# TensorE sums w_val's low parts, w_out's first piece is loaded and converted later, the last rests get a buffer of their own

## The chip, the cores and the metric

One core of a Trainium2 chip runs the whole program; the other cores are idle. The metric is the device time of one execution in microseconds (us). The kernel before takes 745.67 us in the median of three runs (744.39 to 746.3).

## What is computed

Three layers follow each other for 8 batches of 576 tokens, 512 features (8 heads of 64).

```python
# 1 linear attention with an RMS norm over each head
kv  = einsum('bhsd,bhse->bhde', k, v)
out = einsum('bhsd,bhde->bhse', q, kv)
x   = out / sqrt(mean(out**2, -1) + 1e-6) * g_norm          # heads put side by side
# 2 gate: a causal convolution of 5 taps in time, a product with w_val, w_out
gate = sigmoid(sum_k conv_w[k] * shift(x, k))
y    = (gate * (x @ w_val)) @ w_out
# 3 spatial gating
h    = gelu(y @ w_in); u, v = split(h)
v    = (v - mean(v)) / sqrt(var(v) + 1e-6) * g_ln
out  = y + (u * (w_sg @ v + b_sg)) @ w_out2
```

The weights come as 64-bit floats. TensorE multiplies fp32r operands; to keep precision, every operand is split into a high part (rounded to fp32r) and a low part (the rest), and a product is three matmuls: high by high, low by high, high by low.

## The kernel before

**Layout.** Features lie on the 128 partitions in four pieces (m = 0 to 3), tokens along the free dimension: 512 main tokens of each batch, and the 64 tokens left over ("rests") of four batches together. Layers 1 and 2 run batch by batch and store y to DRAM (y_main, y_rest); layer 3 runs over the batches again.

**Weights of 64 bits.** A piece of w_val or w_out is 128 columns by 512 rows, 512 KB. `split` (line 131) makes its two parts out of the raw words. On ACT, `first` takes the absolute value of the high word (L117) and later a copy rounds the high part into the weight (L162, to WV or WOh). On DVE there are seven steps of 128x512: the sign (L127), a minimum (L128), the high part put together (L120), its exponent (L129), the low word scaled (L124), the high part less its rounded copy (L167), and the sum of the last two, which is the weight's low part (L169, to WV or WOl). `in_turn` (line 657) runs two pieces, step by step in turn. The pieces of w_val and w_out use two scratch buffers (m % 2) in the tile wiv.

**The start of the program**, inside `tc.manual_schedule()`, stands in the order in which it is written: the loads on SP's queue; both pairs of w_val; 40 dummy products (`busy`, L217, tile warm) on TensorE; the k by v products (L252) in two halves; the first piece of w_out; the conv weights (cw); then batch 0's attention. For each of its five token tiles: q by kv (L268, tile o), the square on ACT (L275), its sum over a head (L278) and a scale (L279) on DVE, the power -1/2 on POOL (L280), the scaling on DVE (L283), a transpose on TensorE (L298, tile xT), two copies on ACT (L302, L303), and the low part of x on DVE (L307). After it come the products with w_val (tile val), the convolution (16 steps L332 on DVE, tile G), the gate (L360), the split of the gated value (tile Z: L361, L364), and w_out's second piece.

**Behind it a scheduler** sets the order on every engine, by its own idea of the times. An engine works through its queue in that order. The products with w_out (tile y) need w_out's pieces: y's feature piece m needs the high and low part of piece m. Pieces 2 and 3 of w_out are split in that part, among batch 1's attention and convolution.

**The end.** Layer 3's last step for a batch is `wout2`: 12 matmuls (tile out), DVE adds y to half of it (L586, in the tile Y that y was loaded to), SP stores it (L587). After the last batch the rests of the last four batches follow: y_rest is loaded to Y (L877), of which there is one buffer.

Of the kernel before, what the change touches and what calls it, by code (L numbers as in the profile page):

```python
# [10 lines left out]
F32R = mybir.dt.float32r  # L11
# [8 lines left out]
P = 128  # L20
# [40 lines left out]
def body(ctx, tc, qT, k, v, gcol, w_val, conv_w, w_out, w_in, g_ln, w_sgT, b_sg, w_out2, out, out_r):  # L61
# [8 lines left out]
    def sb(tag, shape, dtype=F32, bufs=1):  # L70
        count[0] += 1
        return pool.tile([P] + shape, dtype, tag=tag, name=f"{tag}_{count[0]}", bufs=bufs)
# [15 lines left out]
    def f32(x):  # L88
        return x.bitcast(F32)
# [4 lines left out]

    ident = sb("ident", [P])
    make_identity(nc, ident)
    mhalf = sb("mhalf", [8])
    nc.gpsimd.memset(mhalf, -0.5)
    kvbd = [sb(f"kvbd{i}", [NK, P]) for i in range(2)]
# [8 lines left out]
    def wide_parts(raw, t):  # L108

        hi, lo = raw[:, :, 1], raw[:, :, 0]
        m, b, s = t[:, 0], t[:, 1].bitcast(I32), t[:, 2].bitcast(I32)

        def first():
            act(m, hi.bitcast(F32), AF.Abs, scale=2.0 ** -112)  # L117

        def high():
            stt(b, m.bitcast(I32), 3, s, op0=ALU.logical_shift_left, op1=ALU.bitwise_or)  # L120
            return f32(b)

        def low():
            stt(m, lo.bitcast(U32), 2.0 ** -52, f32(s), op0=ALU.mult, op1=ALU.mult)  # L124
            return m

        return first, (lambda: ts(s, hi, -0x80000000, None, op0=ALU.bitwise_and),  # L127
                       lambda: ts(m, m, EXP_MAX, None, op0=ALU.min), high,  # L128
                       lambda: ts(s, b, -0x800000, None, op0=ALU.bitwise_and), low)  # L129

    def split(src, h, l, raw=None, tmp=None, k=None, on_pool=True):

        st = {}
        n = src.shape[1] * (k or 1)
        wide = src.dtype != F32

        def flat(x):
            return x.rearrange("p (k n) -> p k n", k=k) if k else x

        def load():  # L140
            r = raw
            if r is None:
                r = sb("raw", [WC * 2], I32 if wide else F32, bufs=2)
            if not wide:
                r = r.bitcast(F32)[:, :n] if raw is not None else r[:, :n]
            st["raw"] = r
            s = src.bitcast(I32) if wide else src
            dma(flat(r), s.rearrange("(k p) n -> p k n", p=P) if k else s)

        def first():  # L150
            if wide:
                st["steps"] = wide_parts(st["raw"].rearrange("p (n t) -> p n t", t=2),
                                         sb("cv", [3, n]) if tmp is None else tmp)
                st["steps"][0]()

        def steps():

            ops = st["steps"][1]
            yield ops[0]()
            yield ops[1]()  # L160
            a = ops[2]()
            act(h, flat(a), AF.Copy)  # L162
            yield
            yield ops[3]()
            c = ops[4]()
            yield
            (nc.gpsimd.tensor_tensor if on_pool else tt)(flat(a), flat(a), f32(h), op=ALU.subtract)  # L167
            yield
            tt(l, flat(a), flat(c), op=ALU.add)  # L169
            yield  # L170

        def rest():
            r = st["raw"]
            if wide:
                for _ in steps():
                    pass
            else:
                act(h, flat(r), AF.Copy)
                tt(l, flat(r), f32(h), op=ALU.subtract)

        def work():
            first()
            rest()

        return load, work, first, steps if wide else lambda: iter([rest()])

    def split_weight(w, src, c0, n):

# [26 lines left out]
    def busy(n):  # L215
        for i in range(n):
            nc.tensor.matmul(warm[:, :P], lhsT=ident, rhs=ident, start=True, stop=True)  # L217
# [411 lines left out]

    spare = sb("Y", [2, 2 * D], I32)  # L630

    def first_weight(w, src, raws):
        return [split(src[:, m * P:(m + 1) * P], w[0][:, :, m * P:(m + 1) * P], w[1][:, :, m * P:(m + 1) * P],
                      raws[m], first[1][:, m % 2], NK, False)
                for m in range(NK)]

    wv_pieces = first_weight((wv[:, 0], wv[:, 1]), w_val, [first[0][:, i] for i in range(4)])
    wo_pieces = first_weight(wo, w_out, [spare[:, 0], spare[:, 1], first[0][:, 0], first[0][:, 1]])
    att = Attention(0)
    atts = [att, Attention(1)]  # L640

# [14 lines left out]

    def in_turn(*pieces):

        for p in pieces:
            p[2]()  # L660
        running = [p[3]() for p in pieces]
        while running:
            running = [r for r in running if next(r, running) is not running]


    with tc.manual_schedule():
        for m in range(NK):
            wv_pieces[m][0]()
        wo_pieces[0][0]()
        att.load_kv()  # L670
        dma(gcol_s, gcol)
        dma(gln_s, g_ln)
        cw_work = taps()
        att.load_q()
        atts[1].load_kv()
        wo_pieces[1][0]()
        atts[1].load_q()
        in_turn(wv_pieces[0], wv_pieces[1])
        in_turn(wv_pieces[2], wv_pieces[3])
        wo_pieces[2][0]()  # L680
        wo_pieces[3][0]()
        busy(40)
        att.kv(0)
        busy(5)
        att.kv(1)
        busy(4)
        in_turn(wo_pieces[0])
        slots.drain()
        cw_work()
        steps = [att.o(t, None) for t in range(5)]  # L690
        lows = []
        for t in range(5):
            steps[t][0](ts)
            if t >= 2:
                steps[t - 2][1]()
                busy(4)
                lows.append(steps[t - 2][2]())
            if t == 4:
                lows[0]()
        for t in (3, 4):  # L700
            steps[t][1]()
            if t == 3:
                busy(4)
                lows.append(steps[t][2]())
            lows[t - 2]()
        lows[3]()
        moe = Moe(att.xh, att.xl, gate, y_main[0])
        steps[4][2]()
        for m in range(NK):
            att.taps(m)  # L710
        z = [moe.val(m, True) for m in (0, 1)]
        atts[1].kv(0)
        atts[1].kv(1)
        slots.drain()
        z += [moe.val(m, True) for m in (2, 3)]
        for a in (0, 2):
            att.conv((a, a + 1))
            att.sigmoid(a)
            att.sigmoid(a + 1)
        for m in range(NK):  # L720
            z[m][0]()
        for m in range(NK):
            z[m][1](False)
        in_turn(wo_pieces[1])
    marks = [latest()]
    atts.append(Attention(2))
    atts[2].load_kv()
# [99 lines left out]
    for b in range(B):  # L827
        more = b + 1 < B
        if b % RG == 0:
            if b:  # L830
                grp = Group(b // RG, Group.load(b // RG))
            ggr = sb("WOh", [2, NK, RW], F32R)
            for m in range(NK):
                grp.hu(m)
                tick()
        gg = sb("Z", [2, NK, MAIN], F32R)
        for m in range(NK):
            u = toks.hu(m)
            tick()
            vs = tmp(S)  # L840
            for c in range(2):
                sg(b, c, m, toks.v, rem[b % 2], vs)
                if c:
                    gated(b, m, vs, u, grp.u, gg, ggr)
                tick()
            if more and m == 2:
                ntoks = Tokens(b + 1)
                ntoks.load(0)
                ntoks.load(1)
        res = sb("Y", [NK, MAIN])  # L850
        for m in range(NK):
            dma(res[:, m], y_main[b][:, m])
        if more:
            nrem = Rests((b + 1) // 2) if b % 2 else None
            for t in range(4):
                ntoks.split(t)
                if t < 2:
                    ntoks.load(t + 2)
                ntoks.hv(t)
                tick()  # L860
                if t:
                    wout2(t - 1, gg, res, out[b])
                    tick()
            if nrem:
                nrem.split()
                rem = nrem.hv()
                tick()
            wout2(3, gg, res, out[b])
            tick()
        else:  # L870
            slots.drain()
            for m in range(NK):
                wout2(m, gg, res, out[b])
                tick()
        if b % RG == RG - 1:
            res = sb("Y", [NK, RW])
            dma(res, y_rest[b // RG])  # L877
            for m in range(NK):
                wout2(m, ggr, res, out_r[b // RG])
                tick()  # L880
        if more:
            toks = ntoks
# [41 lines left out]
```

## Time and profile before

| | |
|---|---|
| median of three runs | 745.67 us |
| the profiled execution | 744.89 us, its span 743.1 us |
| TensorE (PE) busy | 728.1 us, 98% of the span |
| VectorE (DVE) busy | 588.4 us, 79% |
| ScalarE (ACT) busy | 348.5 us, 47% |
| GpSimd (POOL) busy | 151.7 us, 20% |

The 1.8 us between the span and the execution's time lie around the span and are taken as fixed. TensorE is busy nearly all of the span, so time can be won at the two ends, where it waits, and lost wherever it is made to wait in between. DVE is busy almost without a gap from 5 to 82 us.

### The profile page before, as it was taken

The numbers are of one execution on the slowest core, as the hardware profiler recorded it, in microseconds if no ns is written. First come the engines' busy times: TensorE is split into PE (matmuls) and PEld (weight loads), VectorE is DVE, ScalarE is ACT, GpSimd is POOL, SyncE is SP. The second block draws the span as 40 slices with busy tenths as digits, with TensorE's granted clock in tenths as the row PEclk, the third lists the DMA queues.
The fourth block names the chain that finished last, engine by engine and source line by source line (L and its number), as shares of the span: only waits on it lengthen the run. The fifth ranks groups of instructions, "written<-read, shape, count | busy, mean of one in ns | idle before, by whom it ended". The sixth has DMA issues, their size and how long they took to land.

```text
span 743.1 us, 11758 instructions
## 1 busy us (share of the span) xinstructions
PE 728.1 (98%) x4498; PEld 625.8 (84%) x4498; DVE 588.4 (79%) x1137; ACT 348.5 (47%) x662; POOL 151.7 (20%) x163
## 2 busy tenths in 40 slices
PE   8898999999999999999999999999999999999996
PEld 7787788778878787889989889888899888898896
DVE  6899979898879899699985786766866857867662
ACT  3757465565665665465433433324433424334220
POOL 0405537261626281211000010000100000100000
PEclk9999999999999999999999999999999999999999
DMA  9935243623363111443122211221230122111203
GB/s 293 343 131 192 103 146 135 210 82 139 132 224 121 54 71 71 156 150 118 58 70 71 85 66 39 81 86 53 90 128 29 57 86 70 59 58 43 100 1 113
DMA packets 56199, 80.14 MB, mean 108 GB/s; under 512 B 3664, under 2 KB 29264, under 8 KB 55120
## 3 DMA queue, kind: packets, MB, share of 16 engines
q1 hardware_dynamic: 56144, 79.40, 32.0%
q8 instruction: 35, 0.57, 0.3%
q14 instruction: 20, 0.16, 0.1%
HBM read 60.51 MB, written 18.87 MB: 107 GB/s over the span
## 4 chain that ended last, share of the span: by engine, by line
PE 85%; DVE 9%; POOL 2%; DMA 1%; issue 1%; ACT 1%; SPq 0%; DVEq 0%; POOLq 0%
PE sg L560 16%; PE hv L451 13%; PE out L201 12%; PE hu L201 12%; PE val L201 11%; PE y L201 10%; DVE G L332 4%; PE kv L252 3%; PE o L268 3%; PE xT L298 2%; POOL st L280 2%; PE hur L201 2%; DMA wiu<-in_w_val_dram 1%; DVE st L278 1%; DVE wiv L120 1%
## 5 line engine op out<-in xcount | busy, mean ns | idle before, releaser
L332 DVE SCALAR_TENSOR_TENSOR G<-X,cw,G 128x576 f32<-128x576 f32 x128 | 98.8, 819 | 6.5 <-ACT G L326 6.5
L201 PE MATMUL y<-Z,WOh 128*128 128x512 f32 (+1 forms) x320 | 99.7, 383 | 0.0
L463 POOL TENSOR_TENSOR bmv<-bmv,mhalf 128x1 f32<-128x1 f32 x36 | 21.4, 596 | 344.2 <-DVE bmv L462 344.2
L451 PE MATMUL hv<-wiv,X1h 128*128 128x512 f32 x256 | 83.3, 390 | 0.0
L201 PE MATMUL out<-Z,K 128*128 128x512 f32 x256 | 83.1, 389 | 0.0
L201 PE MATMUL hu<-X1h,wiu 128*128 128x512 f32 x256 | 79.4, 391 | 0.0
L280 POOL TENSOR_TENSOR st<-st,mhalf 128x8 f32<-128x8 f32 (+1 forms) x40 | 73.5, 1846 | 26.0 <-DVE st L279 23.5
L201 PEld LDWEIGHTS y<-Z,WOh 128*128 128x128 f32 x320 | 57.7, 188 | 11.0
L440 ACT ACTIVATE T<-T 128x512 f32<-128x512 f32 x68 | 42.9, 631 | 45.1 <-DVE T L437 44.9
L201 PE MATMUL y<-Z,WOl 128*128 128x512 f32 (+1 forms) x160 | 59.0, 372 | 0.0
L201 PEld LDWEIGHTS out<-Z,K 128*128 128x128 f32 x256 | 48.1, 188 | 10.0
L451 PEld LDWEIGHTS hv<-wiv,X1h 128*128 128x128 f32 x256 | 47.8, 188 | 10.0 <-ACT X1h L428 0.5
L201 PEld LDWEIGHTS hu<-X1h,wiu 128*128 128x128 f32 x256 | 46.6, 188 | 8.3
L561 DVE SCALAR_TENSOR_TENSOR T<-sg,gln,WOl 128x288 f32<-128x288 f32 x64 | 32.7, 516 | 25.7 <-PE sg L560 25.4
L201 PE MATMUL hu<-X1l,wiu 128*128 128x512 f32 x128 | 50.0, 391 | 0.0
L451 PE MATMUL hv<-wiv,X1l 128*128 128x512 f32 x128 | 49.9, 390 | 0.0
L201 PE MATMUL out<-Z,V 128*128 128x512 f32 x128 | 49.8, 389 | 0.0
L572 ACT ACTIVATE Z<-T 128x512 fp32r<-128x512 f32 x32 | 20.1, 631 | 57.7 <-DVE T L571 57.7
L268 PEld LDWEIGHTS o<-kvbd,Q 128*128 128x128 f32 (+1 forms) x320 | 39.2, 180 | 6.4 <-ACT kvbd L261 2.0
L268 PE MATMUL o<-kvbd,Q 128*128 128x128 f32 (+1 forms) x320 | 42.0, 277 | 1.2 <-ACT kvbd L261 1.2
L201 PE MATMUL val<-X1h,WV 128*128 128x512 f32 x128 | 41.3, 403 | 0.4 <-DVE T L360 0.4
L201 PE MATMUL val<-X0h,WV 128*128 128x512 f32 x128 | 41.4, 404 | 0.0
(152 smaller groups left out, 1708.6 us busy)
## 6 DMA issues: line engine op xcount, KB each, us to landing
Q<-in_qT_dram SPq DMA_DIRECT2D x8, 1152.0 KB, 6.3
y_main<-Y SPq DMA_DIRECT2D x8, 1024.0 KB, 3.9
raw<-y_main SPq DMA_DIRECT2D x32, 256.0 KB, 3.1
Y<-y_main SPq DMA_DIRECT2D x32, 256.0 KB, 4.0
out_dram<-Y SPq DMA_DIRECT2D x32, 256.0 KB, 2.3
K<-in_k_dram SPq DMA_DIRECT2D x7, 1024.0 KB, 5.7
V<-in_v_dram SPq DMA_DIRECT2D x7, 1024.0 KB, 9.3
raw<-in_w_in_dram SPq DMA_DIRECT2D x16, 256.0 KB, 5.2
```

Source lines behind the costliest of these rows:

```text
L201: nc.tensor.matmul(ps, lhsT=a[:, kt, msl], rhs=x[:, kt], start=(i == 0), stop=(i == 3 * NK - 1))
L252: nc.tensor.matmul(self.pk[j][h, h], lhsT=self.k[:n, t, js][:, h], rhs=self.v[:n, t, js][:, h], start=(t == 0), stop=(t == 4))
L268: nc.tensor.matmul(po[:n, j * P:(j + 1) * P], lhsT=self.q[:, j, o:o + n], rhs=bd[:, j, :], start=True, stop=True)
L280: nc.gpsimd.tensor_tensor(st[:n, 2], st[:n, 1], mhalf[:n], op=ALU.pow)
L298: nc.tensor.transpose(pt[:, j * P:j * P + n], xo[:n, j * P:(j + 1) * P], ident[:n, :n])
L332: stt(gate[:, m], x32[:, m, j:j + S], cw3[:, m, j:j + 1], gate[:, m], op0=ALU.mult, op1=ALU.add)
L440: act(w, w, AF.Tanh, scale=CG * AG)
L451: nc.tensor.matmul(ps, lhsT=a[:, kt], rhs=p2["wiv"][:, w, kt], start=(i == 0), stop=(i == 3 * NK - 1))
L463: nc.gpsimd.tensor_tensor(mv[:, 3:4], mv[:, 2:3], mhalf[:, 0:1], op=ALU.pow)
L560: nc.tensor.matmul(ps, lhsT=a[:, msl], rhs=w, start=(n == 0), stop=(n == len(mm) - 1))
L561: later(0, lambda: stt(vs[:, sl], ps, gln_s[:, m:m + 1], p2["bsg"][:, sl], op0=ALU.mult, op1=ALU.add))
L572: act(g[:, 0], x, AF.Copy)
```

## The change

1. w_val: the two last DVE steps (L167, L169) of all four pieces are taken away. The scaled low word is written straight into the weight's low place. TensorE then adds three things in PSUM: the full high part times the identity (fp32), the rounded high part times minus the identity, the low word times the identity (both fp32r), 512 columns each; ACT copies the sum to the weight's low place. POOL makes the two identities (tile GR). Pieces 0 and 1 are summed in front of the k by v products, pieces 2 and 3 in place of two of the four groups of 4 dummies between batch 0's transposes; these are copied behind the taps. Pieces 2 and 3 get scratch buffers of their own (tile Z).
2. The dummies are 30, 4, 8 and 8 where they were 40, 5 and 4; the k by v products stand ahead of the second pair on each queue.
3. w_out's first piece: its load stands behind q's, and it is split together with the second piece behind batch 0's gate, not ahead of batch 0's attention.
4. The last rests: y_rest is loaded to a buffer of its own (XR) when the last batch's Y is loaded.

```diff
+    signed = sb("GR", [2, P], F32R)
+    for i, x in enumerate((1.0, -1.0)):
+        nc.gpsimd.tensor_scalar(signed[:, i], ident, x, 0.0, op0=ALU.mult, op1=ALU.add)
...
-            c = ops[4]()
+            c = ops[4]() if last else ops[4](l, flat)
             yield
-            (nc.gpsimd.tensor_tensor if on_pool else tt)(flat(a), flat(a), f32(h), op=ALU.subtract)
+            if last is None:
+                st["parts"] = a, c
+                return
+            last(flat(a), flat(a), f32(h), op=ALU.subtract)
...
+        def summed():
+
+            a, c = st["parts"]
+            ps = bank("l", n)
+            for i, (w, x) in enumerate(((ident, flat(a)), (signed[:, 1], h), (signed[:, 0], c))):
+                nc.tensor.matmul(flat(ps), lhsT=w, rhs=x, start=(i == 0), stop=(i == 2))
+            return lambda: act(l, flat(ps), AF.Copy)
...
-        wo_pieces[0][0]()
         att.load_kv()
-        dma(gcol_s, gcol)
-        dma(gln_s, g_ln)
         cw_work = taps()
         att.load_q()
+        dma(gcol_s, gcol)
+        wo_pieces[0][0]()
+        dma(gln_s, g_ln)
...
+        busy(30)
+        for p in wv_pieces[:3]:
+            p[2]()
         in_turn(wv_pieces[0], wv_pieces[1])
+        for copy in [p[4]() for p in wv_pieces[:2]]:
+            copy()
+        busy(4)
+        att.kv(0)
+        busy(8)
+        wv_pieces[3][2]()
         in_turn(wv_pieces[2], wv_pieces[3])
...
-        busy(40)
-        att.kv(0)
-        busy(5)
+        cw_work()
         att.kv(1)
-        busy(4)
-        in_turn(wo_pieces[0])
         slots.drain()
-        cw_work()
+        busy(8)
...
-                busy(4)
+                if t < 4:
+                    copies.append(wv_pieces[t][4]())
+                else:
+                    busy(4)
...
-        in_turn(wo_pieces[1])
+        for p in wo_pieces[:2]:
+            p[2]()
+        in_turn(*wo_pieces[:2])
...
+        if not more:
+            res_r = sb("XR", [NK, RW])
+            dma(res_r, y_rest[b // RG])
...
-            res = sb("Y", [NK, RW])
-            dma(res, y_rest[b // RG])
+            if more:
+                res_r = sb("Y", [NK, RW])
+                dma(res_r, y_rest[b // RG])
```

What the scheduler makes of it is seen in the order of the built programs. Rows are: line, operation, written tile, read tiles, shape; lines of the changed kernel are numbered anew.

DVE before, behind the split of w_out's pieces 0 and 1, from the sign of piece 2 to the high part of piece 3 (T is batch 1's attention, X1l the low part of its x):

```order
L127 TENSOR_SCALAR wiv_89<-wiu_88 128x512
L128 TENSOR_SCALAR wiv_89<-wiv_89 128x512
L127 TENSOR_SCALAR wiv_89<-wiu_88 128x512
L283 TENSOR_TENSOR T_577<-o_571,st_576 128x512
L307 SCALAR_TENSOR_TENSOR X1l_94<-xT_634,gcol_76,X1h_93 128x4x128
L120 SCALAR_TENSOR_TENSOR wiv_89<-wiv_89 128x512
L128 TENSOR_SCALAR wiv_89<-wiv_89 128x512
L283 TENSOR_TENSOR T_584<-o_578,st_583 128x512
L307 SCALAR_TENSOR_TENSOR X1l_94<-xT_642,gcol_76,X1h_93 128x4x128
L283 TENSOR_TENSOR T_599<-o_593,st_598 64x512
L129 TENSOR_SCALAR wiv_89<-wiv_89 128x512
L120 SCALAR_TENSOR_TENSOR wiv_89<-wiv_89 128x512
```

DVE now, from the low parts of w_out's pieces 0 and 1 to the high part of piece 3 (the last row; L123 is the old L120):

```order
L177 TENSOR_TENSOR WOl_84<-wiv_92 128x4x128 x2
L130 TENSOR_SCALAR wiv_92<-wiu_91 128x512 x2
L323 SCALAR_TENSOR_TENSOR X1l_98<-xT_712,gcol_79,X1h_97 128x4x128
L131 TENSOR_SCALAR wiv_92<-wiv_92 128x512
L348 SCALAR_TENSOR_TENSOR G_86<-X_12_85,cw_81,G_86 128x576 x2
L123 SCALAR_TENSOR_TENSOR wiv_92<-wiv_92 128x512
L348 SCALAR_TENSOR_TENSOR G_86<-X_12_85,cw_81,G_86 128x576 x4
L338 TENSOR_TENSOR XR_615<-X_12_85,XR_615 128x4x64
L131 TENSOR_SCALAR wiv_92<-wiv_92 128x512
L132 TENSOR_SCALAR wiv_92<-wiv_92 128x512
L348 SCALAR_TENSOR_TENSOR G_86<-X_12_85,cw_81,G_86 128x576 x4
L123 SCALAR_TENSOR_TENSOR wiv_92<-wiv_92 128x512
```

Before, piece 3's high part stood ahead of batch 1's convolution; now ten of its steps stand in front of it, and so do both steps L177 of the first two pieces.

TensorE before, where the products with w_out's pieces 2 (y_762) and 3 (y_789) begin:

```order
L298 MATMUL xT_745<-ident_65,T_599 128x64 x4
L201 MATMUL y_762<-Z_399,WOh_80 128x512
L268 MATMUL o_775<-kvbd_3_72,Q_632 128x128 x4
L201 MATMUL y_789<-Z_399,WOh_80 128x512
L268 MATMUL o_802<-kvbd_3_72,Q_632 128x128 x4
L201 MATMUL val_826<-X1h_93,WV_79 128x512 x2
```

TensorE now, at the same place (y_771 is piece 2, y_798 piece 3):

```order
L217 MATMUL y_733<-Z_399,WOh_83 128x512
L217 MATMUL y_771<-Z_399,WOh_83 128x512
L284 MATMUL o_784<-kvbd_4_75,Q_641 128x128 x4
L217 MATMUL y_798<-Z_399,WOh_83 128x512
L284 MATMUL o_811<-kvbd_4_75,Q_641 128x128 x4
L217 MATMUL val_835<-X1h_97,WV_82 128x512 x2
```

The first matmul of piece 3 stands at the same place as before, behind the 24 matmuls of pieces 0 and 1, the transposes and one of piece 2.

## Rows read from the trace of the kernel before

**Rows 1.** The page: busy us, share of the span, instructions of each engine

```profile
PE 728.1 (98%) x4498; PEld 625.8 (84%) x4498; DVE 588.4 (79%) x1137; ACT 348.5 (47%) x662; POOL 151.7 (20%) x163
```

**Rows 2.** Chain at the end: start us, us, what

```profile
731.76 0.70 DVE Y L586
...
732.48 2.29 DMA out_dram<-Y
...
734.85 3.33 DMA Y<-y_rest
```

**Rows 3.** Timeline of the end: start us, us, engine, line, operation, tiles, count [idle before]

```profile
737.12 0.28 PE L201 MATMUL out<-WOh,K 128*128 128x256 f32 x1
738.36 1.42 DVE L586 SCALAR_TENSOR_TENSOR Y<-out,Y 128x256 f32<-128x256 f32 x4 [5.90 <-DMA Y<-y_rest]
738.81 1.80 SPq L587 DMA_DIRECT2D out_dram<-Y  x4
```

**Rows 4.** Timeline of the start, TensorE, ACT and DVE

```profile
2.27 12.09 PE L217 MATMUL warm<-ident 128*128 128x128 f32 x80 [2.27 <-POOL X L207]
14.29 1.15 PE L252 MATMUL kv<-V,K 128*64 128x64 f32 x32
17.92 1.87 PE L252 MATMUL kv<-V,K 128*64 128x64 f32 x48 [1.17 <-DMA V<-in_v_dram]
21.11 0.63 ACT L162 ACTIVATE WOh<-wiv 128x512 fp32r<-128x512 f32 x1 [1.30 <-DVE wiv L120]
23.27 0.22 ACT L261 ACTIVATE kvbd<-kv 64x64 f32<-64x64 f32 x1
24.71 0.68 DVE L278 TENSOR_REDUCE st<-T 128x8 f32<-128x512 f32 x1
25.75 8.08 POOL L280 TENSOR_TENSOR st<-st,mhalf 128x8 f32<-128x8 f32 x5 [23.48 <-DVE st L279]
```

**Rows 5.** Busy time by stretch, warm matmuls (L217): matmuls seen, weight loads, granted clock

```profile
5.00:6.00 1.00, 1.00 (x6) 1.00 (x6) 1.00 1.00 333
11.00:12.00 1.00, 1.00 (x12) 1.00 (x11) 1.00 1.05 387
```

**Rows 6.** Timeline of DVE, 53 to 83 us

```profile
53.75 0.42 DVE L127 TENSOR_SCALAR wiv<-Y 128x512 int32<-128x512 int32 x1
54.08 0.42 DVE L128 TENSOR_SCALAR wiv<-wiv 128x512 f32<-128x512 f32 x1
54.42 1.86 DVE L278 TENSOR_REDUCE st<-T 128x8 f32<-128x512 f32 x3
...
60.12 0.68 DVE L283 TENSOR_TENSOR T<-o,st 128x512 f32<-128x512 f32 x1
60.72 0.67 DVE L169 TENSOR_TENSOR WOl<-wiv 128x512 fp32r<-128x512 f32 x1
...
67.29 0.68 DVE L120 SCALAR_TENSOR_TENSOR wiv<-wiv 128x512 int32<-128x512 int32 x1
67.89 0.74 DVE L307 SCALAR_TENSOR_TENSOR X1l<-xT,gcol,X1h 128x512 fp32r<-128x512 f32 x1
68.55 0.68 DVE L124 SCALAR_TENSOR_TENSOR wiv<-wiu,wiv 128x512 f32<-128x512 uint32 x1
...
79.06 2.99 DVE L332 SCALAR_TENSOR_TENSOR G<-X,cw,G 128x576 f32<-128x576 f32 x4
83.58 0.69 DVE L283 TENSOR_TENSOR T<-o,st 128x512 f32<-128x512 f32 x1 [1.53 <-POOL st L280]
```

**Rows 7.** Timeline of ACT and TensorE where piece 3 of w_out is first used

```profile
68.00 0.63 ACT L162 ACTIVATE WOh<-wiv 128x512 fp32r<-128x512 f32 x1
70.52 0.47 PE L201 MATMUL y<-Z,WOh 128*128 128x512 f32 x1
```

**Rows 8.** Timeline of POOL, the power for batch 2's first two tiles

```profile
78.68 4.86 POOL L280 TENSOR_TENSOR st<-st,mhalf 128x8 f32<-128x8 f32 x1
83.91 1.64 POOL L280 TENSOR_TENSOR st<-st,mhalf 128x8 f32<-128x8 f32 x1
```

More of the change, by code (lines that the diff above doesn't have):

```diff
@@ L121, in high, with low @@
             return f32(b)
-        def low():
-            stt(m, lo.bitcast(U32), 2.0 ** -52, f32(s), op0=ALU.mult, op1=ALU.mult)
-            return m
+        def low(c=m, of=lambda x: x):
+            stt(c, of(lo.bitcast(U32)), 2.0 ** -52, of(f32(s)), op0=ALU.mult, op1=ALU.mult)
+            return c
         return first, (lambda: ts(s, hi, -0x80000000, None, op0=ALU.bitwise_and),
@@ L129, in wide_parts, with split @@
                        lambda: ts(s, b, -0x800000, None, op0=ALU.bitwise_and), low)
-    def split(src, h, l, raw=None, tmp=None, k=None, on_pool=True):
+    def split(src, h, l, raw=None, tmp=None, k=None, last=nc.gpsimd.tensor_tensor):
         st = {}
@@ L183, in work @@
             rest()
-        return load, work, first, steps if wide else lambda: iter([rest()])
+        return load, work, first, steps if wide else lambda: iter([rest()]), summed if wide and last is None else lambda: lambda: None
     def split_weight(w, src, c0, n):
@@ L630, in body, with first_weight @@
     spare = sb("Y", [2, 2 * D], I32)
-    def first_weight(w, src, raws):
+    more = sb("Z", [2, 3, D])
+    tmps = [t[:, i] for t in (first[1], more) for i in range(2)]
+    def first_weight(w, src, raws, tmps, last):
         return [split(src[:, m * P:(m + 1) * P], w[0][:, :, m * P:(m + 1) * P], w[1][:, :, m * P:(m + 1) * P],
-                      raws[m], first[1][:, m % 2], NK, False)
+                      raws[m], tmps[m], NK, last[m])
                 for m in range(NK)]
-    wv_pieces = first_weight((wv[:, 0], wv[:, 1]), w_val, [first[0][:, i] for i in range(4)])
-    wo_pieces = first_weight(wo, w_out, [spare[:, 0], spare[:, 1], first[0][:, 0], first[0][:, 1]])
+    wv_pieces = first_weight((wv[:, 0], wv[:, 1]), w_val, [first[0][:, i] for i in range(4)], tmps, [None] * 4)
+    wo_pieces = first_weight(wo, w_out, [spare[:, 0], spare[:, 1], first[0][:, 0], first[0][:, 1]],
+                             tmps[:2] * 2, [tt] * 4)
     att = Attention(0)
@@ L657, in in_turn @@
     def in_turn(*pieces):
-        for p in pieces:
-            p[2]()
         running = [p[3]() for p in pieces]
@@ L681, in body @@
         wo_pieces[3][0]()
-        busy(40)
-        att.kv(0)
-        busy(5)
+        cw_work()
         att.kv(1)
-        busy(4)
-        in_turn(wo_pieces[0])
         slots.drain()
-        cw_work()
+        busy(8)
         steps = [att.o(t, None) for t in range(5)]
+        copies = []
         lows = []
@@ L710, in body @@
             att.taps(m)
+        for copy in copies:
+            copy()
         z = [moe.val(m, True) for m in (0, 1)]
@@ L875, in body @@
         if b % RG == RG - 1:
-            res = sb("Y", [NK, RW])
-            dma(res, y_rest[b // RG])
+            if more:
+                res_r = sb("Y", [NK, RW])
+                dma(res_r, y_rest[b // RG])
             for m in range(NK):
-                wout2(m, ggr, res, out_r[b // RG])
+                wout2(m, ggr, res_r, out_r[b // RG])
                 tick()
```

## The prediction, made before the changed kernel ran

> **What bounds the kernel now.** I read the page first, then the chain of waits at the end, then the timelines of the start and of the stretch from 53 to 84 us, and laid the changed order on them. The page says that TensorE is busy 98% of the span [rows 1]. So between the two ends nothing is won, and each us for which TensorE is made to wait is lost. The two ends are where it waits already.
>
> At the end, the last product is done at 737.12 + 0.28 = 737.40 us, but DVE can add y to it only at 738.36, since it waited 5.90 us for the load of the rests [rows 3]. The chain tells why: the one buffer Y had to be stored (2.29 us) before it was loaded again (3.33 us) [rows 2]. Four additions (1.42 us) and four stores, issued in 1.80 us, follow, and all of it stands behind the last product [rows 3].
>
> At the start, DVE works from 5 us on, and batch 0's first sum over heads starts at 24.71 us [rows 4]. From there on POOL's five powers follow each other without a gap for 8.08 us [rows 4]; they set the pace of batch 0's attention.
>
> **The end (part 4).** The rests' y is loaded some 150 us earlier than it is needed, to a buffer last read by the rests' own products, so it is there. DVE takes up a product within 0.05 us (the last main one at 731.76 [rows 2]). The last addition then runs from 737.45 for 0.42 us (a quarter of 1.42, and its last has nothing behind it), and the last store is issued at 737.9. Before, the fourth issue began at about 738.81 + 3 x 0.45 = 740.2 [rows 3], and the span ended 2.9 us later, at 743.1. So the end comes at 740.8: **2.3 us won**. Bounds: 1.9 if the store takes 0.4 longer, 2.6 if four stores that are now spread out land sooner. SP gets the load between the Y load of batch 4 and the next tokens, where nothing waits for it.
>
> **The start (parts 1 and 2, and the removed piece).** DVE loses two steps of 0.60 us in each of four pieces (60.12 to 60.72 is the distance of two such steps [rows 6]), 4.8 us, and the seven steps of w_out's first piece, 3 x 0.34 + 4 x 0.60 = 3.4 us (0.34 is 53.75 to 54.08 and on to 54.42 [rows 6]). That is 8.2 us of an engine without a gap. But the sum over heads needs the product with kv, and that path runs over TensorE, so I count TensorE's queue:
> - 30 dummies in place of 40 (two passes each, 80 in the row [rows 4]): 20 passes less at 0.11, done at 14.29 - 2.1 = 12.2.
> - Two sums. One fp32 product of 512 columns is four times one of 128, so 8 passes of 0.11, 0.9 us; the two fp32r products are below the 0.47 of one from start to end [rows 7], and overlap: 0.3 each. 2 x 1.5 = 3.0: 15.2. This is an estimate; no such sum is in the trace.
> - 4 dummies 0.9, the first k by v half 1.15, 8 dummies 1.8, the second half 1.87 [rows 4], and 8 dummies 1.8: 22.7. The load of v, for which the second half waited until 17.92 [rows 4], is earlier by w_out's piece and in time.
> - ACT copies kv out from 21.0 in 8 steps of 0.23 (the last took 0.22 [rows 4]), to 22.8. Before, these copies stood behind the rounding of w_out's piece, which ended at 21.74, and were done at 23.49 [rows 4].
>
> So the product with q comes 0.5 us or so earlier, not 8: behind DVE, TensorE is late next. From there POOL's powers take as long as before. The sums of pieces 2 and 3 (1.5 us each) replace dummies of 0.9 beside them, and cost 0.1 on ACT's copies. **0.4 us won.** Bounds: sums twice as long give 2.6 lost; sums at half that, 1.5 won.
>
> **The piece that moves (part 3).** Its seven steps come back behind batch 0's gate, where DVE has no gap either. What that costs depends on which step TensorE waits for. The first product with piece 3 has the same place in TensorE's queue as before; behind it, all of batch 1's products. Before, ACT rounded piece 3 at 68.00, done at 68.63, and TensorE came to it at 70.52 [rows 7]: 1.9 us in hand. Now DVE's row from the first step of pieces 0 and 1 to the high part of piece 3 holds, counted in the order:
> - 11 short steps (signs, minima, exponents) of 0.34: 3.7
> - 19 of the 0.60 kind (4 sums over heads, of which three took 1.86 in a row; 5 scalings; 4 high parts, 2 low words, 2 differences, 2 low parts of pieces 0 to 3): 11.4
> - 4 low parts of x at 0.66 (67.89 to 68.55): 2.6
> - 10 convolution steps at 0.73 (a quarter of 2.99 less an overlap of 0.08), and the rests' split 0.34: 7.6
>
> Together 25.4 us, all from [rows 6]. The same stretch before, 53.75 to the end of 67.29 + 0.68, was 14.2. The stretch begins 0.4 earlier by the start and 0.6 later since one sum over heads now stands ahead of it: 53.95. Piece 3's high part is there at 79.4, its rounded copy, 0.63 later [rows 7], at 80.1. TensorE comes to it having done the same products as before, and waits until 80.1 where it was 70.52 before: **9.6 us lost**. Of these some 6 stand in one gap right ahead of it, the rest in the transposes and the products with piece 0, whose low part is done later too. Behind it, all work on TensorE is as before, so nothing is won back. The low parts of pieces 2 and 3 come 5.7 us (seven or so steps) later each, at 85 and 91, while TensorE has 6 and 11 us of other products to do; they just fit. Bounds: 4 (if the scheduled convolution steps run beside waits that I take for filled) to 12 (if those low parts are late by 2).
>
> **Sum.** 744.89 - 2.3 - 0.4 + 9.6 = 751.8 by the profiled execution. It lies 0.8 below the median of the runs, 745.67, so I say **752.6**.
>
> **A page weighed.** DVE waited 1.53 us for a power that took 4.86 us, while the next one took 1.64 [rows 6, 8]; the long one lay beside a row of convolution steps. The Trainium skill, "SBUF — State Buffer", section "Who interferes with whom", says that a DVE instruction with two SBUF inputs and a GpSimd one that reads SBUF block each other wholly. By that rule the same power, now issued at about 83 among convolution steps, would end at 88 or later, and DVE's scaling, due at 88, would wait up to 1.6 us; that would make the sum at most 0.8 higher. The rows alone bound it the same way, and it is inside the range.
>
> **Rivals.**
> 1. *TensorE's clock falls in the new gap.* From 3 to 8 us, after standing idle, TensorE got through 6 or 7 warm matmuls per us, and 12 from 9 us on, with the granted clock shown as 1.00 in both [rows 5]; about 2.6 us were lost in 5.7. After gaps of 1.2 us [rows 4] nothing like it is seen. The gap of 6 us lies between these. If the loss returned in full, the time is 755.2. The Trainium skill, "TensorE: Matmul & The Clock Gate", section "What's actually happening", says that an idle stretch puts the clock to its lower level of 1.2 GHz and that work raises it to 2.4 GHz again; by it this rival would be the forecast. Chance 0.35.
> 2. *Faster.* The wait for piece 3 doesn't arise because DVE's convolution steps, or what they wait for, let piece 3 pass early enough: if its high part is rounded by 70.1, TensorE waits for nothing new and the two ends remain, 745.67 - 2.7 = 743.0. Against it: an engine's order is fixed when the program is built, and DVE has 25 us of work in that row. Chance 0.07.
> 3. *No change.* Only the moved work itself shows: piece 3 late by 3.4 + 0.6 - 0.4 = 3.6 us, less the 1.9 in hand, gives 1.7 lost; other DVE waits (1.53 at 83.58 [rows 6]) take up the rest. 745.67 - 2.7 + 1.7 = 744.7. Chance 0.08.
> 4. *Slower still.* The sums on TensorE take twice as long or the second low parts are late: 757 and above. Chance 0.07.
>
> My forecast has 0.43. What a measurement of this kernel can tell from no change is about 0.3%, 2.2 us. Slower by over 0.3% (above 747.9): the forecast, rivals 1 and 4, 0.85. Within: 0.08. Faster: 0.07. The range takes the forecast's bounds below (4 in place of 9.6 gives 747.2, most of it lies above 748.5) and rival 1 above with some spread: 748.5 to 757. Outside are rivals 2, 3 and 4.
>
> **What would show it.** Right: a gap of 5 us or more of TensorE near 74 to 80 us, ended by ACT's rounded copy of w_out; DVE without a gap from 54 to 80; the first sum over heads at about 24.2; the rests' additions each right behind their product, with none of the 5.90 us wait, and 2.9 us from the last issue to the end; from 110 us on, the same rows some 9 us later. Wrong: TensorE at the first product of piece 3 before 74 us; the first sum over heads before 21 (then TensorE's queue was shorter than counted) or after 26; warm-like slow matmuls right behind the gap (rival 1).

## The result, and the profile after

The changed kernel takes **754.26 us** in the median of four runs (753.84 to 755.47); the kernel before takes 745.04 us beside it. The ratio is 1.0124, with a 95% interval of 1.0104 to 1.0145: slower by 1.2%. A second set of runs gave 754.59 us and 1.0128. The forecast was 752.6 us, in a range of 748.5 to 757. All medians below count every run; the ratios leave out one run of 2512.88 us, of the eleven of experiment 7, whose median without it is 743.88.

The profiled execution has a span of 752.9 us, 9.8 more than before. The page and the view of the cores (us, mean granted TensorE clock) say where not to look: TensorE is busy 98% as before [rows 1], but 7.7 us longer for as many instructions (4500, 4498 before), at a mean clock of 0.989 (0.999 before). Of TensorE's costliest groups of matmuls (busy, mean ns of one, idle before them), the products with w_out are the one with a wait that before had none. The first two lines are of the changed kernel, the last is of the kernel before:

```profile
PE 735.8 (98%) x4500; PEld 630.4 (84%) x4500; DVE 584.1 (78%) x1129; ACT 350.3 (47%) x666; POOL 154.2 (20%) x165
...
L217 PE MATMUL y<-Z,WOh 128*128 128x512 f32 (+1 forms) x320 | 101.8, 389 | 4.1 <-ACT WOh L167 4.1
```

```profile
L201 PE MATMUL y<-Z,WOh 128*128 128x512 f32 (+1 forms) x320 | 99.7, 383 | 0.0
```

**The stretch where the time goes.** The timelines of DVE, ACT and TensorE (start us, us, engine, line, operation, tiles, count, idle before and what ended it) between 53 and 81 us; lines are those of the changed kernel:

```profile
53.20 0.76 DVE L130 TENSOR_SCALAR wiv<-Y 128x512 int32<-128x512 int32 x2
...
60.68 0.69 DVE L299 TENSOR_TENSOR T<-o,st 128x512 f32<-128x512 f32 x1 [0.61 <-POOL st L296]
...
66.87 1.27 DVE L177 TENSOR_TENSOR WOl<-wiv 128x512 fp32r<-128x512 f32 x2
68.08 0.74 DVE L130 TENSOR_SCALAR wiv<-wiu 128x512 int32<-128x512 int32 x2
...
78.64 0.68 DVE L123 SCALAR_TENSOR_TENSOR wiv<-wiv 128x512 int32<-128x512 int32 x1
...
79.35 0.63 ACT L167 ACTIVATE WOh<-wiv 128x512 fp32r<-128x512 f32 x1 [2.78 <-DVE wiv L123]
...
65.09 1.12 PE L314 MATMUL xT<-ident,T 128*128 128x128 f32 x4 [2.55 <-DVE T L299]
...
80.03 0.79 PE L217 MATMUL y<-Z,WOh 128*128 128x512 f32 x1 [4.09 <-ACT WOh L167]
```

The signs of pieces 2 and 3 (L130, `wiv<-wiu`) start only after the low parts of pieces 0 and 1 (L177, 66.87), because they use the same scratch (experiment 5 takes that away). Ten convolution steps then stand between them and piece 3's high part at 78.64. TensorE stops for 4.09 us until ACT has rounded it. The product that started at 70.52 before [rows 7] starts at 80.03: 9.5 us later.

**The clock behind the gap.** Busy time in stretches of the changed kernel (stretch in us, its length, then each engine's busy time with the instructions seen, granted TensorE clock, DMA share, GB/s). A clock of 1.00 is 2.4 GHz, 0.50 is 1.2 GHz:

```profile
60.00:65.00 5.00, 1.51 (x7) 0.81 (x5) 4.38 (x9) 3.12 (x6) 4.55 (x4) 0.64 1.02 386
65.00:70.00 5.00, 4.56 (x15) 3.46 (x16) 5.00 (x11) 3.76 (x7) 0.00 (x0) 0.50 0.22 62
70.00:75.00 5.00, 5.00 (x21) 3.97 (x20) 5.00 (x8) 3.18 (x7) 0.00 (x0) 0.84 0.00 0
...
77.00:79.00 2.00, 0.00 (x0) 0.00 (x0) 2.00 (x4) 0.00 (x0) 0.00 (x0) 0.86 0.00 0
79.00:81.00 2.00, 0.97 (x3) 0.87 (x4) 2.00 (x4) 0.63 (x1) 0.00 (x0) 0.50 0.00 0
...
83.00:85.00 2.00, 2.00 (x6) 1.52 (x6) 2.00 (x5) 0.80 (x2) 2.00 (x1) 0.50 0.00 0
85.00:87.00 2.00, 2.00 (x12) 1.69 (x11) 2.00 (x4) 0.63 (x1) 1.92 (x2) 0.93 0.00 0
87.00:95.00 8.00, 8.00 (x45) 6.76 (x45) 5.95 (x11) 3.20 (x7) 6.68 (x5) 1.00 0.00 0
```

The clock falls twice. First around 60 to 65 us, where TensorE works 1.51 us of 5 between its waits for DVE's scalings; it is up again in the course of 70 to 75. It falls again inside the 4.09 us gap and stays at 0.50 until 85. The first fall makes the products with pieces 0 and 1 slow, but TensorE would otherwise only have waited longer for piece 3, since DVE's row runs on without a gap from 60.68. The second has nothing behind it to hide in. From 87 us on the clock stays at 1.00, and the same rows come 11.5 to 11.8 us later than before.

**The start and the end.** Timelines of TensorE, ACT and DVE at the start [rows 4], then of TensorE, DVE and SP at the end [rows 3]:

```profile
2.27 9.10 PE L233 MATMUL warm<-ident 128*128 128x128 f32 x60 [2.27 <-POOL X L223]
11.21 1.02 PE L185 MATMUL l<-wiv,ident 128*128 128x512 f32 x2
...
12.54 1.02 PE L185 MATMUL l<-wiv,ident 128*128 128x512 f32 x2
...
21.49 4.75 PE L284 MATMUL o<-kvbd,Q 128*128 128x128 f32 x40
...
23.21 0.69 DVE L294 TENSOR_REDUCE st<-T 128x8 f32<-128x512 f32 x1 [3.45 <-ACT T L291]
...
748.90 0.28 PE L217 MATMUL out<-WOh,K 128*128 128x256 f32 x1
...
749.22 0.42 DVE L602 SCALAR_TENSOR_TENSOR XR<-out,XR 128x256 f32<-128x256 f32 x1 [0.99 <-PE out L217]
...
745.42 4.59 SPq L603 DMA_DIRECT2D out_dram<-XR  x4
```

The first sum over heads starts 1.5 us earlier than before (24.71 [rows 4]). At the end the last addition runs 0.04 us behind its product, and 3.7 us lie between the last product's end (749.18) and the end of the span, where it was 5.7. So the account of the profile is: piece 3 late by 9.5, another 2.3 until the last product (749.18 against 737.40), 2.0 won at the end: 9.8.

### The profile page after: what moved, and what is told of

It reads as the page before. It is cut to its first block, busy times and chain, and to the rows that moved or that the text cites. A ratio compares the mean times of both kernels' runs of the same rounds, so it can differ in the third digit from the quotient of the medians.

```text
span 752.9 us, 11753 instructions
## 1 busy us (share of the span) xinstructions
PE 735.8 (98%) x4500; PEld 630.4 (84%) x4500; DVE 584.1 (78%) x1129; ACT 350.3 (47%) x666; POOL 154.2 (20%) x165
## 4 chain that ended last, share of the span: by engine, by line
PE 89%; DVE 7%; POOL 1%; ACT 1%; DMA 1%; issue 1%; POOLq 0%; SPq 0%; DVEq 0%
PE sg L576 16%; PE out L217 13%; PE hv L467 13%; PE val L217 12%; PE hu L217 12%; PE y L217 10%; DVE G L348 4%; PE kv L268 3%; PE o L284 3%; PE xT L314 2%; PE warm L233 2%; PE hur L217 2%; DMA raw<-y_main 1%; PE l L185 1%; POOL st L296 0%
## 5 line engine op out<-in xcount | busy, mean ns | idle before, releaser
L217 PE MATMUL y<-Z,WOh 128*128 128x512 f32 (+1 forms) x320 | 101.8, 389 | 4.1 <-ACT WOh L167 4.1
L467 PE MATMUL hv<-wiv,X1h 128*128 128x512 f32 x256 | 83.5, 391 | 0.1
L217 PE MATMUL out<-Z,K 128*128 128x512 f32 x256 | 83.1, 389 | 0.0
L217 PE MATMUL hu<-X1h,wiu 128*128 128x512 f32 x256 | 79.4, 391 | 0.0
L296 POOL TENSOR_TENSOR st<-st,mhalf 128x8 f32<-128x8 f32 (+1 forms) x40 | 72.1, 1806 | 23.9 <-DVE st L295 21.3
L217 PEld LDWEIGHTS y<-Z,WOh 128*128 128x128 f32 x320 | 58.9, 191 | 15.6 <-ACT WOh L167 4.3
L217 PE MATMUL y<-Z,WOl 128*128 128x512 f32 (+1 forms) x160 | 59.9, 377 | 0.3 <-DVE WOl L177 0.3
L217 PEld LDWEIGHTS out<-Z,K 128*128 128x128 f32 x256 | 48.1, 188 | 10.1
L217 PEld LDWEIGHTS hu<-X1h,wiu 128*128 128x128 f32 x256 | 46.6, 188 | 8.3
L577 DVE SCALAR_TENSOR_TENSOR T<-sg,gln,WOl 128x288 f32<-128x288 f32 x64 | 32.7, 515 | 25.7 <-PE sg L576 25.4
L217 PE MATMUL hu<-X1l,wiu 128*128 128x512 f32 x128 | 50.0, 391 | 0.0
L217 PE MATMUL out<-Z,V 128*128 128x512 f32 x128 | 49.8, 389 | 0.0
L217 PE MATMUL val<-X1h,WV 128*128 128x512 f32 x128 | 42.4, 412 | 0.0
L217 PE MATMUL val<-X0h,WV 128*128 128x512 f32 x128 | 41.4, 404 | 0.0
```

The source lines that it names most:

```text
L217: nc.tensor.matmul(ps, lhsT=a[:, kt, msl], rhs=x[:, kt], start=(i == 0), stop=(i == 3 * NK - 1))
L296: nc.gpsimd.tensor_tensor(st[:n, 2], st[:n, 1], mhalf[:n], op=ALU.pow)
L467: nc.tensor.matmul(ps, lhsT=a[:, kt], rhs=p2["wiv"][:, w, kt], start=(i == 0), stop=(i == 3 * NK - 1))
L577: later(0, lambda: stt(vs[:, sl], ps, gln_s[:, m:m + 1], p2["bsg"][:, sl], op0=ALU.mult, op1=ALU.add))
```

## The experiments

Parts are numbered as in the section on the change. All times are medians, with the ratio to the kernel before run beside them.

**1. The end alone.** The kernel before with part 4.

```
+        if not more:
+            res_r = sb("XR", [NK, RW])
+            dma(res_r, y_rest[b // RG])
...
-            res = sb("Y", [NK, RW])
-            dma(res, y_rest[b // RG])
+            if more:
+                res_r = sb("Y", [NK, RW])
+                dma(res_r, y_rest[b // RG])
...
```

> The kernel before with part 4 alone: the last rests' y loaded to a buffer of its own. Theory (the stores and the load of the one buffer are what stands behind the last product, and nothing else in the change touches the end): 2.0 us less than before, as the stretch from the last product to the span's end fell from 5.7 to 3.7 us between the two traces; 743.0, and the same trace up to 730 us. Rival (the end was shortened by how the changed kernel arrives there): no gain, 745.

**742.36 us**, ratio 0.9965 (0.9952 to 0.9978); the span is 740.8, 2.3 less than before. Its timeline of TensorE and DVE at the end:

```profile
737.06 0.28 PE L201 MATMUL out<-WOh,K 128*128 128x256 f32 x1
...
737.38 0.42 DVE L586 SCALAR_TENSOR_TENSOR XR<-out,XR 128x256 f32<-128x256 f32 x1 [0.99 <-PE out L201]
```

Each addition waits only for its product. Part 4 does what the forecast says of it, and of all kernels here this one has the lowest median.

**2. The move alone.** The kernel before with part 3: w_out's first piece loaded behind q and split together with the second. Two small loads (gcol, gln) go behind q with it, as in the full change.

```
-        wo_pieces[0][0]()
         att.load_kv()
-        dma(gcol_s, gcol)
-        dma(gln_s, g_ln)
...
+        dma(gcol_s, gcol)
+        wo_pieces[0][0]()
+        dma(gln_s, g_ln)
...
-        in_turn(wo_pieces[0])
...
-        in_turn(wo_pieces[1])
+        in_turn(*wo_pieces[:2])
```

> The kernel before with part 3 alone: w_out's first piece loaded behind q and split together with the second behind batch 0's gate; w_val as before. Theory (the move is the whole loss: TensorE waits for piece 3, whose split stands behind ten convolution steps): batch 0's first sum over heads at about 21.5 us, 3 earlier than before, since DVE loses 3.4 us there; then a gap of 4 to 6 us on TensorE ahead of the first product of piece 3, ended by ACT's copy of w_out, and a lower clock behind it; 752 to 755. Rival A (the loss needs TensorE's sums or their scratch in the tile Z): 742, no gap above 2 us. Rival B (only the 3.4 us of work show up, less the 3 won ahead of it): 745 to 746.

**754.97 us**, ratio 1.0140 (1.0122 to 1.0157). TensorE and DVE:

```profile
20.98 5.39 PE L268 MATMUL o<-kvbd,Q 128*128 128x128 f32 x40 [0.35 <-DMA Q<-in_qT_dram]
...
23.34 0.69 DVE L278 TENSOR_REDUCE st<-T 128x8 f32<-128x512 f32 x1 [1.71 <-ACT T L275]
...
79.80 0.50 PE L201 MATMUL y<-Z,WOh 128*128 128x512 f32 x1 [3.21 <-ACT WOh L162]
```

Two things follow. The move alone costs 10 us, with the same wait for the same rounded copy, so the sums on TensorE have no part in it. And the first sum over heads is at 23.34: not the 3 us earlier that were expected, but within 0.13 of the full change. So nearly all of the 1.5 us that the start gains comes from taking w_out's piece out of it, not from the sums. One thing that stands in the way there is the load of q: the product with q waited for it, 0.35 us here, and 1.65 us, until 22.93, in the kernel of experiment 1, where w_out's piece is loaded first. It isn't the only one. In the trace of the kernel before, whose start is the same as experiment 1's, ACT's copy of kv came last, at 22.12. The row of experiment 1, then that of the kernel before:

```profile
22.93 4.83 PE L268 MATMUL o<-kvbd,Q 128*128 128x128 f32 x40 [1.65 <-DMA Q<-in_qT_dram]
```

```profile
22.12 5.60 PE L268 MATMUL o<-kvbd,Q 128*128 128x128 f32 x40 [1.25 <-ACT kvbd L261]
```

**3. Everything but the move.** The full change with part 3 undone; the second half of the k by v products (`att.kv(1)`) goes back ahead of the split, as in the kernel before.

```
+        wo_pieces[0][0]()
         ...
-        wo_pieces[0][0]()
...
+        att.kv(1)
+        wo_pieces[0][2]()
+        in_turn(wo_pieces[0])
+        slots.drain()
         cw_work()
-        att.kv(1)
-        slots.drain()
...
-        for p in wo_pieces[:2]:
-            p[2]()
-        in_turn(*wo_pieces[:2])
+        wo_pieces[1][2]()
+        in_turn(wo_pieces[1])
```

> The changed kernel with part 3 undone: w_out's first piece loaded and split where it was before. Theory (part 3 is the loss): no gap above 3 us on TensorE, clock at full speed from 10 us on, 742 to 746; what the sums win at the start is eaten up by the split that stands ahead of the attention again. Rival (the sums on TensorE or the new places of the loads lose time too): 748 or above.

**745.05 us**, ratio 0.9999 (0.9987 to 1.0011). TensorE and DVE:

```profile
23.44 4.83 PE L284 MATMUL o<-kvbd,Q 128*128 128x128 f32 x40 [0.91 <-DMA Q<-in_qT_dram]
...
73.12 0.79 PE L217 MATMUL y<-Z,WOl 128*128 128x512 f32 x1 [2.13 <-DVE WOl L177]
...
25.23 0.69 DVE L294 TENSOR_REDUCE st<-T 128x8 f32<-128x512 f32 x1 [0.70 <-ACT T L291]
```

The 9 us are gone, which agrees with experiment 2. But the end's 2.6 us, which experiment 1 measured, are gone too. DVE is freed of w_val's last steps, and the load of q holds the product up until 23.44 instead: the first sum over heads comes 0.5 us later than before, not earlier. A wait of 2.13 us for a low part of w_out follows, and behind it the clock falls, which wasn't expected: 0.78 in the mean of 70 to 75 us. Parts 1 and 2, without part 3, cost 2.7 us by the medians (745.05 less 742.36; the two intervals lie apart). But the ten runs lie in two groups of five: 743.96 to 744.21 us at a mean clock of 1.00, and 745.89 to 746.67 at 0.997 or 0.998. Over experiment 1 that is 1.6 to 1.9 us in the one and 3.5 to 4.3 in the other. The profiled execution, 746.67, is the longest of the second group; what the first group waits for was not traced. Parts 1 and 2 were not run apart from each other.

**4. The gap filled.** The full change, with 18 dummy products placed where TensorE stands idle for piece 3, behind the product that it did last. Their results aren't used.

```
+            if b == 0 and s == 6:
+                behind([last_pe()], lambda: busy(18))
```

> The changed kernel with 18 dummy products (36 passes, some 3.9 us) put on TensorE in the gap ahead of the first product of piece 3. Their results are not used. Theory (the clock falls because TensorE stands idle there): the granted clock stays at full level from 72 to 87 us, the products behind the gap run at their usual distance of 0.23 us, and the time is 2 to 2.5 us less than the changed kernel's, 751.8 to 752.3. Rival (the slow products behind the gap have another cause, or the time they lose is given back later): 754.3, no change.

**752.04 us**, ratio 1.0095 (1.0081 to 1.0109), against 754.26 and 754.59 for the full change. TensorE and the stretches behind:

```profile
75.68 4.18 PE L233 MATMUL warm<-ident 128*128 128x128 f32 x36
79.95 0.50 PE L217 MATMUL y<-Z,WOh 128*128 128x512 f32 x1
...
75.00:80.00 5.00, 4.91 (x45) 4.72 (x43) 5.00 (x10) 1.58 (x3) 0.00 (x0) 1.00 0.01 3
80.00:85.00 5.00, 5.00 (x30) 4.40 (x31) 5.00 (x9) 1.81 (x3) 2.42 (x1) 1.00 0.00 0
```

The product with piece 3 starts at 79.95, 0.08 from the full change: ACT's copy is done at 79.90 there (79.27 + 0.63). Behind the gap the clock is what differs, 1.00 where it was 0.50, and the kernel is 2.2 to 2.6 us faster. That is the price of the second fall, told apart from the wait itself.

**5. Own scratch for pieces 2 and 3.** The full change; w_out's last two pieces no longer share their scratch with the first two. `owns` are places of raw words that are no longer needed, and a row more each.

```
-                             tmps[:2] * 2, [tt] * 4)
+                             tmps[:2] + owns, [tt] * 4)
```

> The changed kernel, but pieces 2 and 3 of w_out get scratch of their own (dead raw words of w_val and two more 512-column blocks), where they had to wait for the scratch of pieces 0 and 1. The work of every engine is the same. Theory (what costs is the place of the split in DVE's row, which the shared scratch sets: piece 2 can't start before piece 0 is finished at 67.5 us): the rounded copy of piece 3 is done before 75 us, the 4.1 us gap goes, and the time falls by 2 to 5 us, to 749 to 752. Rival (what costs is DVE's total of work, 3.4 us more ahead of batch 1's attention, whatever its order): the wait shows up at another product, and the time stays within 1 us of 754.

**749.85 us**, ratio 1.0064 (1.0048 to 1.0080). The gap at 80 us is gone, and TensorE waits later, for a low part:

```profile
76.16 0.48 PE L217 MATMUL y<-Z,WOh 128*128 128x512 f32 x1
...
86.73 0.50 PE L217 MATMUL y<-Z,WOl 128*128 128x512 f32 x1 [1.83 <-DVE WOl L177]
```

So 4.4 to 4.7 us of the loss, the second fall of the clock among them, came from the place in DVE's row that the shared scratch forces on piece 3, behind ten convolution steps. The rest stays. Piece 3's first product now starts with no wait of its own, but at 76.16, still 5.6 us later than before [rows 7]. Ahead of it are waits for DVE's scalings and the first fall of the clock, which the wait for piece 3 no longer hides. Ten products with pieces 0 and 1 take 4.43 us there (67.82 to 72.25), and twelve take 2.80 us at the upper clock right behind (72.55 to 75.35): some 2 us lost, an estimate from these rows. Then comes the wait of 1.83 us, for DVE steps that are late too.

**6. The piece back at the start, in DVE's idle time.** As experiment 5, but w_out's first piece is loaded ahead of q again and split at the start, where DVE stands idle in the full change.

```
+        wo_pieces[0][0]()
         ...
-        for p in wv_pieces[:3]:
+        for p in wv_pieces:
...
-        cw_work()
+        wo_pieces[0][2]()
+        in_turn(wo_pieces[0])
...
```

> As the run with own scratch, but w_out's first piece is loaded ahead of q and split in the time in which DVE stands idle in the changed kernel (3.8 us from 11.5, 3.5 us from 19.8), with the absolute value of w_val's fourth piece taken ahead of ACT's copies of the sums. Theory (the sums leave DVE idle at the start, so that the piece is split there for nothing, and the loss was its move): first sum over heads at 23 to 23.5 as in the changed kernel, no gap above 3 us, 741 to 743, faster than both. Rival (the load ahead of q delays the product with q, and so batch 0's attention): first sum over heads at 25 or later, 745 or above.

**743.67 us**, ratio 0.9980 (0.9970 to 0.9990): faster than the kernel before, and still not faster than the end alone (0.9965; the two intervals overlap). Its sums over heads start at 24.26, where 23 to 23.5 was expected: the piece's raw words are there only at 18.66, behind the sums of pieces 0 and 1 on TensorE, and DVE's split of them then stands right ahead of the sums over heads. And one wait with a slow stretch behind it is left. DVE, TensorE and the stretch:

```profile
18.66 0.43 DVE L130 TENSOR_SCALAR wiv<-Y 128x512 int32<-128x512 int32 x1 [4.16 <-DMA Y<-in_w_out_dram]
...
20.27 2.05 PE L233 MATMUL warm<-ident 128*128 128x128 f32 x16
22.16 5.12 PE L284 MATMUL o<-kvbd,Q 128*128 128x128 f32 x40
...
65.72 0.70 PE L314 MATMUL xT<-ident,T 128*128 128x128 f32 x4 [2.55 <-DVE T L299]
...
65.00:70.00 5.00, 4.28 (x14) 3.47 (x15) 5.00 (x10) 2.46 (x5) 0.00 (x0) 0.66 0.45 144
```

**7. Fewer dummies at the start.** w_out's first piece at the start as in experiment 6, with the shared scratch of the full change, and 1, 2 and 2 dummies where the change has 4, 8 and 8.

```
-        busy(4)
+        busy(1)
...
-        busy(8)
+        busy(2)
```

> As the run before it, but with the shared scratch, and 5 dummy products where there were 20 around the k by v products (1, 2 and 2 in place of 4, 8 and 8). Theory (at the start TensorE's own queue sets when the attention begins, as I counted it, its dummies included): the first sum over heads about 1.3 us or more earlier, at 21.5 to 22, and 740 to 742. Rival 1 (the loads of k, v and q set it): unchanged at 23 to 23.5. Rival 2 (with fewer dummies TensorE's clock falls at the start): products with q at half speed, 744 or above.

**744.10 us**, ratio 0.9989 (0.9977 to 1.0002), where 740 to 742 was expected. In this kernel the dummies are not what holds the start up:

```profile
17.28 0.71 PE L233 MATMUL warm<-ident 128*128 128x128 f32 x4
21.99 7.04 PE L284 MATMUL o<-kvbd,Q 128*128 128x128 f32 x40 [4.00 <-ACT kvbd L277]
...
20.00:36.00 16.00, 13.85 (x84) 12.01 (x84) 12.13 (x28) 9.40 (x22) 8.11 (x5) 0.79 1.03 332
```

TensorE is through with its dummies 4.3 us earlier than in experiment 6 (17.28 + 0.71 against 20.27 + 2.05), but the 40 products with q start only 0.2 us earlier, after a gap of 4.00 us that ACT's copy of kv ends, and take 7.04 us in place of 5.12. The clock had fallen: 0.79 in the mean of 20 to 36 us. ACT's copy stands behind its rounding of w_out's piece here (19.60), and that behind the load of the piece, which DVE's split waits for until 17.63. So the run doesn't tell what fewer dummies would do in the full change, where that piece is gone and the product with q follows the dummies at once; that was not run.

**8. The full change once more,** beside experiments 5 to 7.

> The changed kernel once more, as a measure for the others on the same chip: 754.3 within 1 us, a ratio to the kernel before of 1.012.

754.59 us, ratio 1.0128 (1.0110 to 1.0146), as before within the intervals.

## Why the prediction was right, and where its terms were off

**The mechanism held.** The forecast puts piece 3's high part at 79.4 and its first product at 80.1; they were at 79.32 and 80.03. It names the releaser (ACT's rounded copy), and the move alone shows the same loss (experiment 2). Rows far behind come 11.5 us later where it says some 9 (one row of k by v products at 137.99 for 126.44); the difference is the clock's share.

**The likeliest case was not the one that came.** The forecast gave 0.43 to a clock that stays up and 0.35 to rival 1, a clock that falls in the gap. It fell. Rival 1's 2.6 us were measured as 2.2 to 2.6 (754.26 and 754.59 less 752.04). With the gap filled, and so without the fall, the kernel takes 752.04, close to the forecast's 752.6; with the fall 754.26, nearer to rival 1's 755.2. The forecast rested on gaps of 1.2 us that had left the clock alone [rows 4] and on the start of the program, with nothing between; behind the gap of 4.09 us it fell.

The Trainium skill, "TensorE: Matmul & The Clock Gate", section "What's actually happening", says that an idle stretch puts the clock to 1.2 GHz. The trace agrees: 0.50 from 79 to 85 us behind the gap. Its rule was named in the prediction and would have been the better choice.

**Part of the nearness is luck.** By the profiled execution the prediction's sum gave 751.8 us, and 754.67 was measured. The 2.9 us between them are the clock (2.3), the start's 0.4, which the sum takes twice, and 0.3 that the end won less, with 0.1 the other way at piece 3. The medians lie closer, 752.6 and 754.26, because the forecast added 0.8 for a profiled execution that lay below its median, while this one lies 0.4 above its own.

**The gap was shorter than foretold,** 4.09 and not 5 us or more. The products ahead of it ran at the lower clock from about 65 to 71 us and filled part of it. The wait for piece 3 ends at the same time either way, so this costs nothing.

**DVE's row.** 25.4 us were counted from the first step to the end of piece 3's high part; 26.1 were taken (53.20 to 79.32). 0.61 of the difference is a wait for POOL that the count has not. The row began at 53.20 where 53.95 was said, so the two errors cancel.

**The start.** 0.4 us were predicted, 1.5 gained at the first sum over heads (23.21 for 24.2). TensorE's queue, counted to 22.7, was through at 21.49. The sums start at 11.21 and not at 12.2, since 20 passes of dummies less save 3.0 us and not 2.1 (60 take 9.10, 80 took 12.09 [rows 4]), and one sum takes 1.33 us (11.21 to 12.54) and not 1.5. As counted, the queue does set the start of the full change: the product with q follows the dummies without a wait. But the account is incomplete, since experiment 2 comes within 0.13 us with no sum on TensorE. It left out the load of q. By its issue and its time to landing, q is there at 20.2 to 21.3 us in the five traces in which w_out's piece is loaded behind it, and at 21.7 to 23.3 in the five in which the piece is loaded ahead of it. And the gain doesn't reach the end of the program. The end alone (2.6 won) and the move alone (10.0 lost) together make 752.4 us; the full change lies 1.9 to 2.2 us above that, about as much as the three intervals leave open. By the traces, whose spans give 1.9 as well, 0.23 of it is piece 3's time (80.03 against 79.80). More comes from a longer stay at the lower clock: in the kernel with the move alone about 80 to 83.5 us, in the full change 79 to 85. The same products with q then start at 98.44 in the one and at 99.52 in the other, 1.1 us apart. Another 0.4 lies at the end: from the last product to the end of the span the full change takes 3.7 us, where the move alone takes 5.55 and part 4, in experiment 1, takes 2.2 off. The rest was not placed. Stretches, and that row, of the kernel with the move alone, and the row of the full change:

```profile
80.00:81.00 1.00, 1.00 (x6) 0.96 (x6) 1.00 (x3) 0.00 (x0) 0.00 (x0) 0.60 0.00 0
...
83.00:84.00 1.00, 1.00 (x4) 0.76 (x3) 1.00 (x3) 0.31 (x2) 1.00 (x1) 0.70 0.00 0
...
98.44 1.09 PE L268 MATMUL o<-kvbd,Q 128*64 128x128 f32 x8
```

```profile
99.52 1.09 PE L284 MATMUL o<-kvbd,Q 128*64 128x128 f32 x8
```

The sum of the prediction also takes the start's 0.4 twice: once in the time at which DVE's row begins, and once as a term of its own. Without that it would have been 753.0. Its lower bound of 747.2, too, is 747.0 by its own numbers (752.6 less 5.6).

**The end.** 2.3 us predicted; 2.3 by the span and 2.6 by the median where it stands alone, 2.0 in the full change. The last issue is at 749.7 (745.42 + 4.59 - 0.33) and the end 3.2 later, not 2.9; in experiment 1 it was 3.0.

**The power on POOL.** The prediction said that the power among the convolution steps would make DVE's scaling wait up to 1.6 us. POOL and DVE:

```profile
85.84 3.88 POOL L296 TENSOR_TENSOR st<-st,mhalf 128x8 f32<-128x8 f32 x1
...
89.76 0.69 DVE L299 TENSOR_TENSOR T<-o,st 128x512 f32<-128x512 f32 x1 [1.53 <-POOL st L296]
90.09 1.64 POOL L296 TENSOR_TENSOR st<-st,mhalf 128x8 f32<-128x8 f32 x1
```

It took 3.88 us where the next one took 1.64, and DVE waited 1.53. The Trainium skill, "SBUF — State Buffer", section "Who interferes with whom", says that a DVE instruction with two SBUF inputs contends with a GpSimd one that reads SBUF, and that the second of them is blocked until the first is done; the rows agree. It cost TensorE no wait, since it had other products to do.

**Rivals 2, 3 and 4** fall. TensorE does wait for piece 3 (against 2 and 3), the sums take 1.33 us and not twice 1.5, and there is no wait for the low parts of pieces 2 and 3 behind 81 us (against 4); with own scratch such a wait appears (experiment 5).

## What to carry to other kernels

Work that is moved off the start of a program to a stretch where the same engine is full can cost more than its own length: here 3.4 us of DVE steps cost 10 us, 4.4 to 4.7 of it in the full change by a scratch shared with what follows. Read from the order of that engine at which of the moved steps the bounding engine next waits, and count the row up to that step. Where the count leaves TensorE a gap of several us, add the price of the lower clock behind it, 2.2 to 2.6 us here. Try the parts of a change alone: here one of four parts won 0.35%, and the others took it back.

## What the runs showed of the hardware

- TensorE's clock fell without one long gap: in the full change it was at 0.69 over 61 to 62 us and at 0.50 over 62 to 63, after waits of 1.53 and 1.03 us with a few transposes between them. It also fell around single waits of 2.13 us (experiment 3) and 2.55 us (experiment 6), and not around one of 1.66 us (experiment 7).
- Eighteen dummies, 4.18 us of work whose results nobody reads, won 2.2 to 2.6 us, because they kept the clock at 1.00.
- At the start a gap of 4.00 us behind too few dummies made the 40 products with q take 7.04 us in place of 5.12.
- In the profiled execution of the kernel with own scratch, the granted clock stood at 0.95 in stretch after stretch in which TensorE was busy without a pause, from 10 us on, between the two levels and near the upper one. The three other runs of that kernel have 0.992 or 0.993 in the mean. Its matmuls took as long as those of the full change (389 ns in both in the group `out<-Z,K`), so nothing in this document rests on it; why it is shown is open. One stretch:

```profile
300.00:320.00 20.00, 20.00 (x95) 16.37 (x94) 16.40 (x35) 10.19 (x21) 5.10 (x5) 0.95 0.30 100
```
